# Attention and experts on one core: the last 64 tokens of q and k turned by four transposes, five additions moved behind the mean scores, 34 unread products added

## The chip, the cores and the metric

One core of a Trainium2 chip runs the whole program. The metric is device time in microseconds (us) for one execution, the median over runs. TensorE is called PE here, VectorE DVE, ScalarE ACT, GpSimd POOL and SyncE SP. SP computes nothing in this kernel; it issues most of the transfers between HBM and on-chip memory.

## The reference, cut to what matters

For 8 batches of 8 heads, 576 tokens of 64 elements each, in float32:

```
q_d, k_d, v_d = means of q, k, v over groups of 4 tokens        # 144 groups
out_d  = softmax(q_d k_d^T / 8) v_d                             # 144 x 144 per head
out_up = each row of out_d repeated 4 times
out_local = softmax over |i - j| < 4 of (q k^T / 8), times v    # a band
x = (out_up + out_local), as 4608 tokens of 512
route: logits = x w_gate; every token goes to one of 8 experts, 576 tokens each, in order of logit
out[token] = relu(x w1[e]) w2[e]
```

## The kernel before, in words

The attention part works in 36 units of 128 tokens (four windows of 32), eight batches of four and a half units. For each batch, q and k are loaded with tokens on partitions (`nat`, and `natt` for the last 64 tokens of a batch, because 576 = 4 x 128 + 64), and turned on PE so that head elements lie on partitions (`qt`, `kt`). The first 512 tokens go by pieces of four 128 x 128 transposes (`trw`). The last 64 go by `trt`, one piece per batch: `natt` holds 16 groups of four tokens times four head pairs on 64 partitions for q and 64 for k, and eight f32 products with the identity turn it; the profile counts each as two PE instructions (`L360`, 16 of them a batch). Two copies, one for q and one for k, then bring the 256 columns of PSUM into `qt` and `kt` (`L328` on DVE or `L330` on ACT, which alternate or are set by `TRV`).

POOL or DVE forms the sums over four tokens (`gsum`). The mean attention of a batch (`down`) is three score steps s0, s1, s2 (products on PE; on DVE a row maximum, `L387`, and a subtraction, `L389`; on ACT the exponentials, `L395` to `L398`), then three steps t0, t1, t2 of transposes on PE (`L411`), then the products with v. Local attention of a unit is scores (`L554`), transposes (`L577`) and products with v (`L598`). `log_a(u)` adds the mean rows of a unit to its local rows (`L608`, on DVE for units under 27), `store(u)` writes the sum to HBM through SP, and `log_t`, `log_m` make the logits.

The order of all this is written out by hand: every piece has a due time in units, and pieces are emitted in order of due time, so that each engine runs its own instructions in that order. `LOC` gives the lag of each stage behind its unit; the addition of unit u is due at u + 4.425, its store at u + 4.6. The score and transpose steps of the mean attention of a batch are spread over `DW` = 0.15 to 1.9 units behind the batch's first unit, nine steps. The turning pieces of the next batch are spread between them, so that the last-64 piece of batch b stands on PE just ahead of the t0 step of batch b - 1; it is called trt(b) here. Loads on SP are `paced`: each waits for a DVE instruction emitted shortly before it.

The function `keep` issues products of a constant tile that nothing reads. `KEEP` = (36, 46) places 36 of them ahead of the transposes of the first unit and 46 ahead of the first turning piece of batch 1. All of the PSUM tiles of these stages come from one pool of six banks (`g`).

After the attention come routing and the eight experts (from about 246 us of the span on), which the diff does not touch.

Of the kernel before, what the change touches and what calls it, by code (L numbers as in the profile page):

```python
# [6 lines left out]
F32 = mybir.dt.float32  # L7
# [10 lines left out]
B, H, S, D = 8, 8, 576, 64  # L18
HD = H * D
HP = H // 2  # L20
# [6 lines left out]
GM = 128  # L27
GT = G - GM
# [22 lines left out]
FL = 4  # L51
EXS = (3,)
TRV = (2, 6)
FT = 3
FTS = {0: 5}
UF1 = 29
# [9 lines left out]
NG = 6  # L66
# [30 lines left out]
TX = 0.0  # L97
VX = 0.0
NWARM = 13
KEEP = (36, 46)  # L100
EV0 = (0,1)
EVV = ((3, 1, 1), (4, 1, 1), (6, 1, 1))
EN0, EN1 = 19, 28
# [12 lines left out]
class Attention:  # L116
# [109 lines left out]
    def load_nat(self, b, which, hh=None):  # L226

        nc = self.nc  # L230
        src = {"q": self.q, "k": self.k, "v": self.v}
        tail = 4 * GM * D
        if which == "t":
            t = self.wk.tile([128, 2, 4, D], F32, name="natt", bufs=1)
            for i, w in enumerate("qk"):
                for j in range(2):
                    nc.sync.dma_start(
                        t[64 * i:64 * i + 64, j].rearrange("p f d -> p (f d)"),
                        bass.AP(tensor=src[w].tensor, offset=src[w].offset + (b * H + j) * S * D + tail,
                                ap=[[4 * D, GT], [2 * S * D, HP], [1, 4 * D]]))  # L240
        elif which == "w":
            t = self.wk.tile([128, 4, D], F32, name="natw", bufs=1)
            nc.sync.dma_start(t.rearrange("p f d -> p (f d)"),
                              bass.AP(tensor=self.v.tensor, offset=self.v.offset + b * H * S * D + tail,
                                      ap=[[S * D, H], [4 * D, GT], [1, 4 * D]]))
        else:
            if (which, b) not in self.nat_:
                self.nat_[which, b] = self.ld.tile([128, H * 4 * D], F32, name="nat").rearrange(
                    "p (h f d) -> p h f d", f=4, h=H)
            t = self.nat_[which, b]  # L250
            h0, h1 = (0, H) if hh is None else (2 * hh, 2 * hh + 2)
            nc.sync.dma_start(t[:, h0:h1].rearrange("p h f d -> p h (f d)"),
                              bass.AP(tensor=src[which].tensor, offset=src[which].offset + (b * H + h0) * S * D,
                                      ap=[[4 * D, GM], [S * D, h1 - h0], [1, 4 * D]]))
        self.nat[which, b] = t
# [97 lines left out]
    def trt(self, b):  # L353

        nc = self.nc
        src = self.nat["t", b]
        p = self.ps.tile([128, 4, 2, GT, HP], F32, name="g", bufs=NG)
        for f in range(4):
            for s in range(2):
                nc.tensor.matmul(p[64 * s:64 * s + 64, f].rearrange("p w g h -> p (w g h)"), src[:, s, f], self.ident,  # L360
                                 start=True, stop=True)
        for i, w in enumerate("qk"):
            t = self.dest(b, w)[:, :, 4 * GM:].rearrange("p h (g f) -> p f g h", f=4)
            self.evac(t, p[:, :, i], i, b in TRV)

    def down_s(self, b, part):
        nc = self.nc  # L370
# [31 lines left out]
    def down_t(self, b, part):  # L402
        nc = self.nc
        self.need(("d", b, part))
        t = self.sd
        if part == 0:
            self.ptd[b] = self.wk.tile([128, 11, 128], F32, name="ptd", bufs=1)
        out = self.ptd[b]
        p = self.ps.tile([128, 512], F32, name="g", bufs=NG)
        for j in range(3):  # L410
            nc.tensor.transpose(p[:, 128 * j:128 * j + 128], t[:, 3 * part + j, :GM], self.ident)  # L411
        self.evac(out[:, 3 * part:3 * part + 3].rearrange("p a b -> p (a b)"), p[:, :384], vector=(b, part) == (0, 1))
# [262 lines left out]
    def run(self, after, ready):  # L675
# [15 lines left out]
        for b in range(B):  # L691
            u0, up = 9 * b // 2, 9 * (b - 1) // 2
            t = self.transposes(b)
# [36 lines left out]
        for u in range(NT):  # L730
# [5 lines left out]
            for j, (name, lag) in enumerate(LOC.items()):  # L736
# [9 lines left out]
                    at += {"t": TX, "v": VX, "v0": VX, "v1": VX}.get(name, 0.0)  # L746
                if name == "add" and u == NT - 1:
                    continue
                if name == "st" and u >= NT - XB:
                    at = max(at, STE + 0.001 * u)  # L750
                if name == "up":
# [899 lines left out]
```

## Time and profile before

| what | value |
|---|---|
| median of 3 runs (lowest to highest) | 690.15 us (687.77 to 691.06) |
| time of the profiled execution | 690.15 us |
| its span, first to last instruction | 688.2 us |
| PE, DVE, ACT, POOL busy share of the span | 94%, 74%, 49%, 36% |
| mean granted clock of PE | 0.979 |
| PE products, and as many weight loads | 8843 |

The profiled execution has the time of the median. Busy shares are averages over stages that have different limits, and a busy PE is not PE at its peak: one matmul shows as 0.27 us or so, while four transposes in a row follow one another in less than half a microsecond. A batch's stretch of the attention part is read from the chain of waits and from the timeline instead.

### The profile page before, as it was taken

The numbers are of one execution on the slowest core, as the hardware profiler recorded it, in microseconds if no ns is written. First come the engines' busy times: TensorE is split into PE (matmuls) and PEld (weight loads), VectorE is DVE, ScalarE is ACT, GpSimd is POOL, SyncE is SP. The second block draws the span as 40 slices with busy tenths as digits, with TensorE's granted clock in tenths as the row PEclk, the third lists the DMA queues.
The fourth block names the chain that finished last, engine by engine and source line by source line (L and its number), as shares of the span: only waits on it lengthen the run. The fifth ranks groups of instructions, "written<-read, shape, count | busy, mean of one in ns | idle before, by whom it ended". The sixth has DMA issues, their size and how long they took to land.

```text
span 688.2 us, 21717 instructions
## 1 busy us (share of the span) xinstructions
PE 646.8 (94%) x8843; PEld 453.2 (66%) x8843; DVE 511.8 (74%) x1475; ACT 333.8 (49%) x648; POOL 248.8 (36%) x332
## 2 busy tenths in 40 slices
PE   7899999989999957999999999999999999999993
PEld 4677888778787845765764764764764764755841
DVE  5787889869879987997888897896896966534500
ACT  4677877678586513525325434424424424433410
POOL 4797486656937413106005104103114026111011
PEclk9999999999999967999999999999999999999997
DMA  8978879877987724506439268068078089623001
GB/s 250 241 195 235 232 188 254 222 194 190 232 230 172 222 72 123 193 13 227 144 118 288 48 221 208 25 245 184 24 259 170 25 280 262 224 47 92 1 31 39
DMA packets 132620, 113.90 MB, mean 165 GB/s; under 512 B 81191, under 2 KB 110119, under 8 KB 132521
## 3 DMA queue, kind: packets, MB, share of 16 engines
q1 hardware_dynamic: 124760, 89.71, 46.7%
q0 software_dynamic: 6752, 22.03, 10.1%
q8 instruction: 70, 1.15, 0.7%
q10 hardware_dynamic: 1008, 0.77, 0.4%
q14 instruction: 30, 0.24, 0.1%
HBM read 85.94 MB, written 19.46 MB: 153 GB/s over the span
## 4 chain that ended last, share of the span: by engine, by line
PE 55%; issue 17%; DVE 13%; ACT 4%; POOL 4%; DMA 3%; SPq 1%; POOLq 0%; ACTq 0%; DVEq 0%
PE pX L1439 17%; PE pH L1391 13%; PE g L598 4%; PE g L346 3%; PE s L554 2%; PE pR L934 2%; PE g L577 2%; POOL out_dram L1449 2%; PE g L618 2%; DVE wl L1310 2%; POOL xg L1327 1%; DMA nat<-in_q_dram 1%; DVE qt L328 1%; PE g L427 1%; PE g L411 1%
## 5 line engine op out<-in xcount | busy, mean ns | idle before, releaser
L1391 PE MATMUL pH<-xt,wh 128*128 128x320 f16 (+2 forms) x1040 | 191.8, 284 | 0.3 <-ACT xt L1348 0.2
L1439 PE MATMUL pX<-wh,ht 128*128 128x512 f16 (+1 forms) x640 | 178.9, 380 | 0.0
L1391 PE MATMUL pH<-xt,wl 128*128 128x320 f16 (+2 forms) x520 | 144.4, 284 | 0.1
L1439 PEld LDWEIGHTS <-ht 128*128 128x128 f16 (+1 forms) x960 | 82.9, 100 | 93.4 <-issue 2.6
L1439 PE MATMUL pX<-wl,ht 128*128 128x512 f16 (+1 forms) x320 | 117.9, 380 | 0.0
L1391 PEld LDWEIGHTS <-wh 128*128 128x128 f16 x1040 | 98.1, 97 | 28.2 <-issue 4.1
L1449 POOL DMA_INDIRECT out_dram<-y,idx x40 | 42.1, 1052 | 172.7 <-ACT y L1446 116.1
L1422 ACT ACTIVATE ht<-pH 128x512 f16<-128x512 f32 (+1 forms) x128 | 45.5, 408 | 114.3 <-PE pH L1391 114.3
L1310 DVE SCALAR_TENSOR_TENSOR wl<-nat,wh 128x512 f16<-128x512 f32 x128 | 83.6, 686 | 15.5 <-ACT wh L1307 13.3
L1446 ACT ACTIVATE y<-pX 128x512 f32<-128x512 f32 (+1 forms) x40 | 23.8, 595 | 102.8 <-PE pX L1439 55.0
L1425 DVE SCALAR_TENSOR_TENSOR ht<-pH,ht 128x512 f16<-128x512 f32 (+1 forms) x128 | 52.4, 450 | 25.6 <-ACT ht L1422 25.1
L1307 ACT ACTIVATE wh<-nat 128x1024 f16<-128x1024 f32 (+1 forms) x68 | 67.6, 1002 | 4.5 <-DMA nat<-in_moe_w_dram 4.5
L1327 POOL DMA_INDIRECT xg<-x_dram,idx x40 | 43.6, 1090 | 62.9 <-DVE idx L1220 48.6
L1391 PEld LDWEIGHTS <-wl 128*128 128x128 f16 x520 | 50.1, 97 | 12.6 <-DVE wl L1310 0.3
L587 ACT COPY pt<-g 64x512 f32<-64x512 f32 x71 | 41.2, 580 | 22.8 <-PE g L577 21.8
L598 PE MATMUL g<-vw,pt 128*64 128x65 f32 x1152 | 43.4, 225 | 2.5 <-issue 1.3
L598 PEld LDWEIGHTS g<-vw,pt 128*64 128x64 f32 x1152 | 37.9, 137 | 8.6 <-issue 5.2
L346 PE MATMUL g<-ident,nat 128*128 128x128 f32 x256 | 39.0, 278 | 2.5 <-DMA nat<-in_q_dram 2.0
L1094 POOL MEMSET f<- 128x1 bf16 x8 | 0.8, 104 | 110.9 <-DVE sumf L988 41.1
L330 ACT COPY kt<-g 64x512 f32<-64x512 f32 (+1 forms) x58 | 36.5, 630 | 7.8 <-PE g L346 6.7
L1356 DVE SCALAR_TENSOR_TENSOR xs<-xg,xs 128x512 f16<-128x512 f32 (+1 forms) x30 | 20.1, 688 | 24.8 <-ACT xs L1355 24.6
L554 PE MATMUL s<-kt,qt 64*32 64x38 f32 x2304 | 29.0, 204 | 5.8 <-issue 5.2
(242 smaller groups left out, 1131.4 us busy)
## 6 DMA issues: line engine op xcount, KB each, us to landing
nat<-in_moe_w_dram SPq DMA_DIRECT2D x28, 1024.0 KB
vw<-in_v_dram SPq DMA_DIRECT2D x136, 78.0 KB
x_dram<-x SPq DMA_DIRECT2D x36, 256.0 KB
nat<-in_q_dram SPq DMA_DIRECT2D x32, 256.0 KB
nat<-in_k_dram SPq DMA_DIRECT2D x32, 256.0 KB
nat<-in_v_dram SPq DMA_DIRECT2D x28, 256.0 KB
up<-up_dram SPq DMA_DIRECT2D x9, 256.0 KB
nat<-in_moe_w_dram POOLq DMA_DIRECT2D x2, 1024.0 KB, 8.7
```

The costliest lines, as they stand in the source:

```text
L346: nc.tensor.transpose(p[:, a, :, fp], src[:, 4 * hh + 2 * a + s, 2 * fp:2 * fp + 2].rearrange("p f d -> p (f d)"), self.ident)
L554: nc.tensor.matmul(sv[32 * hp:32 * hp + 32, i, c], qt[r, hp, QW * w:QW * w + QW], kt[r, hp, key0(w):key0(w) + KW], start=False, stop=True, ...
L587: first = nc.scalar.copy(out[r, :, :, a], src)
L598: nc.tensor.matmul(o[64 * i:64 * i + 64, 65 * h:65 * h + 65], pt[:, 2 * (h % 2) + i, 2 * g + h // 2].rearrange("p b q -> p (b q)"), self.v ...
L1307: self.wh.append(nc.scalar.activation(hi[:, a:b], r[:, a:b], AF.Copy, scale=sc))
L1310: self.wl = nc.vector.scalar_tensor_tensor(lo[:, a:a + LOP], r[:, a:a + LOP], sc, hi[:, a:a + LOP], op0=OP.mult, op1=OP.subtract)
L1327: self.fetched = nc.gpsimd.indirect_dma_start(out=xg[:n], out_offset=None, in_=self.x, in_offset=bass.IndirectOffsetOnAxis(ap=idx[:n, c:c ...
L1391: mm = nc.tensor.matmul(p[:, s, o:o + s1 - s0], w[d][a][:, 128 * f:128 * f + 128], xt[:, b, d, s0:s1], start=j == 0, stop=j == len(seq) - 1)
L1422: last = nc.scalar.activation(hi, q, AF.Relu)
L1425: low = nc.vector.scalar_tensor_tensor(lo, q, 0.0, hi, op0=OP.max, op1=OP.subtract)
L1439: mm = nc.tensor.matmul(p[o:o + m], ht[:, f, h0:h0 + m], w[4 + f // 2][b][:, 512 * (f % 2):512 * (f % 2) + 512], start=j < parts, stop=j > ...
L1449: i = nc.gpsimd.indirect_dma_start(out=self.out, in_=y[:n], in_offset=None, out_offset=bass.IndirectOffsetOnAxis(ap=idx[:n, c:c + 1], axis=0))
```

## The change

Four things change.

- The layout of `natt`: 64 tokens of q on partitions 0 to 63 and 64 of k on 64 to 127, eight heads of 64 elements along the free dimension. It is loaded by two transfers of 512 pieces of 256 bytes, where there were four transfers of 64 pieces of 1 KB.
- `trt` turns it by four 128 x 128 transposes, one for each head pair, and the two copies read runs of 64 consecutive columns and write runs of 64, where they read and wrote single elements with strides before.
- For the units 5, 9, 14, 18 and 23 the addition and the store are due 0.17 units later. The addition was due between the score steps s1 and s2 of the mean attention that runs at that time; it is now emitted behind s2's maximum and subtraction.
- `KEEP` gets a third number: 34 unread products stand ahead of the t1 transposes of batch 0.

```diff
+ADD = {5: 0.17, 9: 0.17, 14: 0.17, 18: 0.17, 23: 0.17}
-KEEP = (36, 46)
+KEEP = (36, 46, 34)
...
         if which == "t":
-            t = self.wk.tile([128, 2, 4, D], F32, name="natt", bufs=1)
+            t = self.wk.tile([128, H, D], F32, name="natt", bufs=1)
             for i, w in enumerate("qk"):
-                for j in range(2):
-                    nc.sync.dma_start(
-                        t[64 * i:64 * i + 64, j].rearrange("p f d -> p (f d)"),
-                        bass.AP(tensor=src[w].tensor, offset=src[w].offset + (b * H + j) * S * D + tail,
-                                ap=[[4 * D, GT], [2 * S * D, HP], [1, 4 * D]]))
+                nc.sync.dma_start(t[64 * i:64 * i + 64],
+                                  bass.AP(tensor=src[w].tensor, offset=src[w].offset + b * H * S * D + tail,
+                                          ap=[[D, S - 4 * GM], [S * D, H], [1, D]]))
...
-        p = self.ps.tile([128, 4, 2, GT, HP], F32, name="g", bufs=NG)
-        for f in range(4):
-            for s in range(2):
-                nc.tensor.matmul(p[64 * s:64 * s + 64, f].rearrange("p w g h -> p (w g h)"), src[:, s, f], self.ident,
-                                 start=True, stop=True)
+        p = self.ps.tile([128, HP, 2, S - 4 * GM], F32, name="g", bufs=NG)
+        for hp in range(HP):
+            nc.tensor.transpose(p[:, hp].rearrange("p w s -> p (w s)"), src[:, 2 * hp:2 * hp + 2].rearrange("p h d -> p (h d)"),
+                                self.ident)
         for i, w in enumerate("qk"):
-            t = self.dest(b, w)[:, :, 4 * GM:].rearrange("p h (g f) -> p f g h", f=4)
-            self.evac(t, p[:, :, i], i, b in TRV)
+            self.evac(self.dest(b, w)[:, :, 4 * GM:], p[:, :, i], i, b in TRV)
...
         p = self.ps.tile([128, 512], F32, name="g", bufs=NG)
+        if (b, part) == (0, 1):
+            self.keep(p, 2)
...
+                if name in ("add", "st"):
+                    at += ADD.get(u, 0.0)
```

## Rows read from the trace of the kernel before

**Rows 1.** The page: PE's granted clock in 40 slices; the instruction queue's packets, MB, share.

```profile
PEclk9999999999999967999999999999999999999997
...
q8 instruction: 70, 1.15, 0.7%
```

**Rows 2.** Chain of waits, 157 to 167 us (start, duration, what): two turning pieces.

```profile
161.00 0.44 PE g L346 x4
...
162.31 1.02 PE g L360 x16
```

**Rows 3.** Groups by form, 0 to 230 us: copies of 256 columns out of PSUM.

```profile
L330 ACT COPY kt<-g 128x256 f32<-128x256 f32 x4 | 2.7, 672 | 0.3 <-DVE kt L328 0.3
...
L328 DVE COPY kt<-g 128x256 f32<-128x256 f32 x4 | 2.5, 626 | 0.0
...
L330 ACT COPY ptd<-g 128x256 f32<-128x256 f32 x6 | 2.3, 376 | 0.0
...
L328 DVE COPY ptd<-g 128x256 f32<-128x256 f32 x2 | 0.8, 424 | 0.0
```

**Rows 4.** Timeline, 13 to 24 us: trt(0)'s follower, trt(1), and SP's issues for it.

```profile
14.67 0.57 PEld L554 LDWEIGHTS s<-kt,qt 64*32 64x32 f32 x54 [0.70 <-ACT kt L330]
...
18.88 1.23 SPq L237 DMA_DIRECT2D natt<-in_k_dram  x2
...
22.64 0.19 PEld L360 LDWEIGHTS g<-ident,natt 128*64 128x64 f32 x2 [0.48 <-DMA natt<-in_q_dram]
...
23.25 0.85 PEld L360 LDWEIGHTS g<-ident,natt 128*64 128x64 f32 x14 [0.42 <-issue]
```

**Rows 5.** Timeline of SP, 26 to 30 us: one load of 312 pieces of 256 bytes.

```profile
27.43 0.31 SPq L277 DMA_DIRECT2D vw<-in_v_dram  x1
```

**Rows 6.** Windows (busy us and count per engine; last: clock, DMA share, GB/s).

```profile
5.00:8.00 3.00, 1.50 (x10) 0.88 (x8) 0.02 (x1) 0.00 (x0) 2.93 (x10) 1.00 1.08 366
...
26.00:28.00 2.00, 2.00 (x23) 1.69 (x22) 1.90 (x6) 1.25 (x2) 1.84 (x3) 1.00 1.16 209
```

**Rows 7.** Timeline, 45 to 48 us: trt(2) on PE.

```profile
45.76 0.19 PEld L360 LDWEIGHTS g<-ident,natt 128*64 128x64 f32 x2 [0.51 <-PE g L384]
...
46.63 0.85 PEld L360 LDWEIGHTS g<-ident,natt 128*64 128x64 f32 x14 [0.69 <-issue]
```

**Rows 8.** Chain of waits, 73 to 82 us: what released t0 behind trt(3).

```profile
77.74 0.63 ACT kt L330
...
78.41 0.55 PE g L411 x3
```

**Rows 9.** Timeline, 104 to 107 us: DVE's subtraction of s2, and t1 behind trt(4).

```profile
105.64 0.61 DVE L389 TENSOR_TENSOR sd<-g,mxd 128x432 f32<-128x432 f32 x1
...
106.36 0.31 PEld L411 LDWEIGHTS g<-ident,sd 128*128 128x128 f32 x3 [0.42 <-ACT kt L330]
```

**Rows 10.** Timeline, 164 to 167 us: DVE's last copy of trt(6), and t2.

```profile
165.17 0.62 DVE L328 COPY kt<-g 128x256 f32<-128x256 f32 x1
...
165.91 0.31 PEld L411 LDWEIGHTS g<-ident,sd 128*128 128x128 f32 x3 [0.31 <-ACT sdt L398]
```

**Rows 11.** Timeline, 192 to 197 us: the addition, and t2 behind trt(7).

```profile
192.77 0.68 DVE L608 TENSOR_TENSOR x<-x,g 128x512 f32<-128x512 f32 x1
...
196.65 0.31 PEld L411 LDWEIGHTS g<-ident,sd 128*128 128x128 f32 x3 [0.38 <-ACT sd L395]
```

**Rows 12.** Windows from the start to the first and last of five stops of PE.

```profile
0.00:19.25 19.25, 13.70 (x219) 9.01 (x219) 9.59 (x21) 8.39 (x14) 8.77 (x26) 1.00 0.86 252
...
0.00:184.65 184.65, 168.71 (x3965) 138.27 (x3966) 147.44 (x372) 132.28 (x264) 125.95 (x192) 1.00 0.83 221
```

**Rows 13.** Who waited for whom on PE, 12 to 245 us (us, times, longest us).

```profile
PE s L554 <- issue: 5.2, 4, 1.8
```

**Rows 14.** Timeline: 46 unread products, and t1 of batch 0.

```profile
19.55 1.64 PE L774 MATMUL g<-wm 128*64 128x64 bf16 x46
...
33.52 0.31 PEld L411 LDWEIGHTS g<-ident,sd 128*128 128x128 f32 x3 [1.32 <-ACT sd L395]
```

## The prediction

> **What bounds the kernel now.** I read the page first, then the chain of waits through the attention part, then the timeline around each of the eight last-64 pieces. The clock line of the page shows full clock through the first fourteen slices, which is the whole attention part [rows 1], so nothing there is waiting to be won by a faster PE clock. The chain says that in most stretches PE runs its pieces back to back: in the stretch of trt(6) four transposes take 0.44 us and the sixteen instructions of the last-64 piece 1.02 us, each beginning where the one before ends [rows 2]. A microsecond taken off PE there is a microsecond off the end. But next to three of the eight pieces PE's next step is released by something else: a copy on ACT behind trt(3) [rows 8], and the same at 135 us behind trt(5), or a load ahead of trt(1) and trt(2) [rows 4, 7]. A saving on PE there only lengthens the wait. So each batch has to be worked out by itself.
>
> **The piece on PE.** Sixteen instructions become eight, in four pairs of load and product of the form of a turning piece: 1.02 - 0.44 = 0.58 us less per batch [rows 2], at most 8 x 0.58 = 4.6 us.
>
> **The copies.** Today a copy of 256 columns with strides takes 672 ns on ACT and 626 ns on DVE; the copies of 256 consecutive columns take 376 and 424 ns [rows 3]. The new copies read and write runs of 64, which no row shows. The bounds are the two pairs of rows; I take the lower end, since both sides of the copy are then runs and not single elements: 0.30 us less per copy on ACT, 0.20 on DVE, two copies a batch. Where these engines are not waited for, this is worth nothing.
>
> **The loads.** SP issues four transfers a batch now, two in 1.23 us [rows 4], so some 2.4 us. A load of 312 pieces of 256 bytes issues in 0.31 us when nothing stands in the way [rows 5]; two of 512 pieces I estimate between 0.6 and 1.2 us. SP waits for its pacing most of the time, so I count this only where trt waits for its load. The transfers themselves get dearer. Windows price both forms: 366 GB/s with pieces of 1 KB alone, 209 GB/s in a window with many pieces of 256 bytes, both with the queues full [rows 6]. For the 256 KB of a batch that is 0.72 against 1.25 us, so 0.5 us more. Early, with the transfer engines full, this takes back most of what SP's quicker issue gives; later the load has several microseconds of lead.
>
> The Trainium skill, DMA: Bandwidth & Descriptors, in its table at the head, asks for at least 512 bytes a piece for line rate and says that smaller ones are read, modified and written; it speaks against this edit. The windows agree in sign: the small pieces move at 209 instead of 366. By that rule, taken as twice the time, I estimate 1.4 us for a batch in place of 0.72.
>
> **The additions.** An addition takes 0.68 us of DVE [rows 11], and moved behind s2 it lets s2's subtraction, the exponentials behind it and t2 come that much sooner. The store on SP goes with it, past the transposes' due times; it waits for the addition anyway and the logits of the unit come a whole unit later, so I price the delay of the addition at nothing (if the store held up the paced loads behind it on SP, by 0.68 and the 0.61 us of a subtraction [rows 9] or so, the loads would have to have less lead than that; only trt(1) and trt(2) show a late one, and neither stands beside a moved addition).
>
> **Batch by batch.**
> - trt(0): the scores behind it wait 0.70 us for copies of other pieces, on ACT [rows 4]. PE's saving is lost: 0, at most 0.2 if the last-64 copy is the one that counts.
> - trt(1): its first load is 0.48 us late and the second stop is 0.42 us [rows 4]. Fewer issues bring the load forward, fuller queues set it back. If it lands as now, the piece still ends 0.58 us sooner; with both waits gone, 1.5 us; with the load 0.9 us later (0.45 for each of two batches), -0.3. I take 0.7.
> - trt(2): the stops are 0.51 and 0.69 us [rows 7], the second for the last of the four loads; with two issues in place of four, SP is through sooner and that wait should go. Up to 0.58 + 1.2 = 1.8; but the same two copies on ACT that release t0 behind trt(3) stand here too, and t0 may wait for them next. I take 0.6.
> - trt(3) and trt(5): t0 starts as the ACT copy ends [rows 8], so PE's saving turns into wait; the shorter copies come behind it. 0 to 0.2 each, together 0.1.
> - trt(4): t1 stands 0.42 us behind DVE's subtraction of s2, which ends at 106.25, and ACT's copies [rows 9]. The addition moved lets that end at 105.57, the copies end 0.6 sooner, and PE is 0.58 sooner: I take 0.6.
> - trt(6): t0 and t1 can start sooner only as far as ACT's exponentials let them; t2 waits 0.31 us, as DVE's copy ends (165.17 + 0.62 = 165.79) [rows 10]. That copy ends 0.4 sooner with both copies short: 0.3 of 0 to 0.9.
> - trt(7): t2 waits 0.38 us for exponentials behind s2 [rows 11]; s2 moves up by 0.68, and PE comes 0.58 sooner. 0.7.
>
> Sum: 0.7 + 0.6 + 0.1 + 0.6 + 0.3 + 0.7 = 3.0 us.
>
> **The unread products.** 46 of them take 1.64 us [rows 14], 0.036 each, so 34 take 1.2 us. PE stands idle for 1.32 us ahead of that t1 [rows 14], so they cost nothing if they start at once. They write the bank that the transposes then use; if that bank comes free only 0.6 us into the wait, they end late by 0.5. The ACT chain that t1 waits for moves with PE, so the cover stays. I take 0, and keep 0.5 for the range.
>
> **The instruction stream.** The instruction queue moved 70 packets and 1.15 MB [rows 1], 16 KB each, for PE's 8843 weight loads and as many products: one packet for about 256. PE stops five times in the attention part for "issue", four of them inside the dense runs of `L554`, 5.2 us together [rows 13]. Counting weight loads from the start, the first stop ends at load 219 and the fifth at 3966 [rows 12]: 3747 apart, 30 times 124.9. All five lie on this grid of about 125 loads (250 instructions and some waits), so these are stops at the end of a fetched block, where a dense run eats it up before the next has come. The change takes 12 loads out at each trt and puts 34 in at batch 0, so the code slides along the grid by -12, -24, +10, -2, and so on to -62. Other places meet the ends of blocks; about as many of them lie in dense runs. I take no change, with 2.5 us either way.
>
> The Trainium skill, Runtime: NRT & Kernel Launch, section Instruction fetch mechanics, has the same 256 instructions a block and says that crossing a block is mostly hidden. The trace differs: 5.2 us of stops in `L554` alone. By that page the slide would change nothing and the sum stays.
>
> **From sum to time.** The profiled execution took 690.15 us with a span of 688.2, so 1.95 us lie outside. It equals the median of the runs. 690.15 - 3.0 = 687.15; rounded, 687.0.
>
> **The rivals.**
> - Part of the gain, as summed: 687.0, within 684.5 to 689.5. Chance 0.50.
> - All of it arrives: PE is the bound everywhere, 4.6 us for the pieces, 1.0 for half of the 2.1 us of stops in trt(1) and trt(2), 1.0 for t1 and t2 (0.42 + 0.31 + 0.38, less a little): 6.6, so 683.5. For it: the chain is mostly PE. Against it: rows 8. Chance 0.22.
> - Almost nothing: DVE and ACT set the pace beside all pieces and the saving turns into waits; 0.7 us, 689.5. For it: rows 8 and 10; against it: t2 at trt(7) [rows 11] is held by the very addition that moves. Chance 0.14.
> - The load comes late: the small pieces cost 0.7 us more per batch and set trt(1) and trt(2) back by 0.7 us each in place of gaining 1.3: 687.0 + 1.3 + 1.4 = 689.7. The full queues of the early part speak for it [rows 6], the lead of the later loads against it. Chance 0.06. This is what the Trainium skill's rule of 512 bytes, cited above, would do.
> - Slower: the slide puts more ends of blocks into dense runs. One such stop costs up to 1.8 us [rows 13]. Two more eat the 3.0 us up; from four more on it is slower: 687.0 + 4 x 1.7 = 693.8. There are 36 dense runs, one a unit, and 3966 / 125 = 32 ends by the fifth stop, so it can happen. Chance 0.08.
>
> **How the numbers follow.** About 0.5%, 3.45 us, is what a measurement of this kernel can tell from no change: its three runs span 3.3 us. Faster by more means under 686.7: the second case and a little under half of the first, 0.22 + 0.22 = 0.44. Slower by more means over 693.6: 0.07, most of the last case. The rest is 0.49. The range runs from 682.8, which leaves out the lower end of the second case, to 691.0, which leaves out the last; 2 in 10 or a little less lie outside.
>
> **What would show it.** In the profile after: the last-64 piece with eight PE instructions a batch, near 0.45 us; its copies near 0.4 us; no load wait ahead of trt(2); t2 behind trt(7) without its wait; t0 behind trt(3) still released by ACT; the 34 products inside the wait ahead of t1, which stays at the exponentials; stops for "issue" at other loads, still on a grid of 125. The prediction is wrong if the waits named fail to swallow PE's saving, if the stops change by more than two, or if the last-64 loads land late.

## The result, and the profile after

The change makes the kernel slower: median 692.15 us against 688.97 for the kernel before, 22 runs each on the same chips; ratio 1.0051, 95% interval 1.0033 to 1.0068. The forecast was 687.0, within 682.8 to 691.0. Ratios here and below leave out runs that took over 1.5% longer than the fastest of their kernel (here one of 22, at 700.90 us), so they differ a little from the quotient of the medians.

The profiled execution of the changed kernel took 696.69 us with a span of 694.9, which is 6.7 us more span than in the profile of before, and lies near the upper end of its runs. So sizes below are read from several traces or from medians, and this one trace only says where to look. The page of the changed kernel, to be held against [rows 1]:

```profile
PEclk9899999999999966999999999999999999999998
...
q8 instruction: 69, 1.13, 0.7%
```

The clock line has a new dent in its second slice, and the low stretch after the attention lies across two slices as before. The queue of instructions moved one packet less, as the shorter code asks.

**What came as forecast.** Groups by form, 0 to 230 us, of the changed kernel: the copies of the last-64 piece.

```profile
L327 DVE COPY qt<-g 128x256 f32<-128x256 f32 x4 | 1.7, 418 | 0.0
L327 DVE COPY kt<-g 128x256 f32<-128x256 f32 x4 | 1.7, 414 | 0.0
L329 ACT COPY kt<-g 128x256 f32<-128x256 f32 x4 | 1.5, 380 | 0.0
L329 ACT COPY qt<-g 128x256 f32<-128x256 f32 x4 | 1.5, 370 | 0.1
```

370 to 380 ns on ACT and 414 to 418 on DVE: at the lower bound of [rows 3], which the forecast took. Timeline of PE's weight loads, changed kernel, around pieces 2, 4, 5 and 7 and the unread products:

```profile
34.72 1.15 PEld L772 LDWEIGHTS <-wm 128*64 128x64 bf16 x34 [0.17 <-issue]
35.91 0.31 PEld L407 LDWEIGHTS g<-ident,sd 128*128 128x128 f32 x3
...
48.40 0.42 PEld L358 LDWEIGHTS g<-ident,natt 128*128 128x128 f32 x4 [0.23 <-issue]
...
107.24 0.62 PEld L594 LDWEIGHTS g<-vw,pt 128*64 128x64 f32 x16 [0.37 <-DVE sd L383]
108.46 0.58 PEld L594 LDWEIGHTS g<-vw,pt 128*64 128x64 f32 x16 [0.60 <-PE g L594]
109.10 0.31 PEld L407 LDWEIGHTS g<-ident,sd 128*128 128x128 f32 x3
...
135.49 0.42 PEld L358 LDWEIGHTS g<-ident,natt 128*128 128x128 f32 x4 [0.23 <-issue]
136.90 0.31 PEld L407 LDWEIGHTS g<-ident,sd 128*128 128x128 f32 x3 [0.99 <-ACT kt L329]
...
194.30 0.42 PEld L358 LDWEIGHTS g<-ident,natt 128*128 128x128 f32 x4 [0.23 <-issue]
194.69 0.36 PEld L407 LDWEIGHTS g<-ident,sd 128*128 128x128 f32 x3
196.01 1.08 PEld L594 LDWEIGHTS g<-vw,pt 128*64 128x64 f32 x32 [0.96 <-ACT kt L329]
197.16 0.31 PEld L407 LDWEIGHTS g<-ident,sd 128*128 128x128 f32 x3
```

The piece is four loads and four products, 0.42 us of loads, where there were sixteen of each. The 34 products take 1.15 us, and t1 behind them starts without a wait, where it had waited 1.32 [rows 14]. The load waits of piece 2 [rows 7] are gone. Behind piece 4 the wait ahead of t1 [rows 9] is gone, but two new ones of 0.37 and 0.60 us stand ahead of it within the products with v. The step behind piece 5 now waits 0.99 us for the copies on ACT, and behind piece 7 the wait ahead of t2 [rows 11] is gone while a new one of 0.96 us for copies stands ahead of the products with v.

**What came otherwise.** PE's weight loads from unit 1 to unit 2, the two units' masks (`identb`) being the first and the last line:

```profile
17.56 0.10 PEld L541 LDWEIGHTS <-identb 64*128 64x128 bf16 x2 [0.17 <-issue]
17.73 0.64 PEld L550 LDWEIGHTS s<-kt,qt 64*32 64x32 f32 x63
21.54 0.13 PEld L550 LDWEIGHTS s<-kt,qt 64*32 64x32 f32 x1 [3.17 <-issue]
25.90 0.70 PEld L358 LDWEIGHTS g<-ident,natt 128*128 128x128 f32 x4
...
33.36 0.10 PEld L541 LDWEIGHTS <-identb 64*128 64x128 bf16 x2 [0.23 <-issue]
```

The same in the kernel before:

```profile
17.58 0.10 PEld L545 LDWEIGHTS <-identb 64*128 64x128 bf16 x2 [0.17 <-issue]
...
19.32 0.18 PEld L554 LDWEIGHTS s<-kt,qt 64*32 64x32 f32 x14 [1.03 <-issue]
...
31.01 0.10 PEld L545 LDWEIGHTS <-identb 64*128 64x128 bf16 x2 [0.22 <-issue]
```

Unit 1 begins when it did before (17.56 against 17.58 us). Its 64 scores stop ahead of the last one for 3.17 us; in the kernel before they stopped ahead of the last fourteen, for 1.03. Unit 2 begins 2.35 us later than before (33.36 against 31.01). Windows of the changed kernel over the same stretch (columns as in [rows 6]; the last three are clock, DMA share, GB/s):

```profile
18.00:20.00 2.00, 0.49 (x52) 0.37 (x30) 0.00 (x0) 0.89 (x2) 1.85 (x4) 0.88 1.01 310
20.00:22.00 2.00, 0.46 (x7) 0.38 (x7) 0.14 (x1) 0.00 (x0) 0.01 (x1) 0.50 0.79 158
22.00:24.00 2.00, 2.00 (x42) 2.00 (x40) 1.93 (x4) 0.00 (x0) 0.00 (x0) 0.50 0.92 286
24.00:26.00 2.00, 2.00 (x16) 1.94 (x15) 0.00 (x0) 0.50 (x1) 1.78 (x3) 0.50 0.82 246
```

While PE stands still its granted clock falls from 2.4 GHz to half, 1.2 GHz, and stays there for 6.8 us, to 26.4. The stop itself is 2.1 us longer than before, which is nearly all of the 2.35; what the half clock adds was not separated, since in the kernel before PE waits for loads in the same stretch [rows 4]. The waits of PE from 12 to 245 us, changed kernel, against [rows 13]:

```profile
PE s L550 <- issue: 8.3, 7, 3.0
```

Seven stops and 8.3 us in the score line, where there were four and 5.2. That line alone misleads: in the kernel before a fifth long stop, 1.22 us, stands in the products with v. Counting all lines, each of the two traces has five stops of more than 0.8 us, 6.9 us in sum before and 7.9 after, and behind unit 1 they fell from 5.8 to 4.7. From unit 2 to the last unit's mask the changed kernel is 0.3 us quicker than before (203.45 against 203.74 us), and from there to the end 4.6 us slower. In this trace the loss lies in two places, then, unit 1 and the end, and between them the gain that was forecast is missing.

### The profile page after: what moved, and what is told of

It is laid out like the page before. It is cut to its first block, busy times and chain, and to the rows that moved or that the text cites. A ratio compares the mean times of both kernels' runs of the same rounds, so it can differ in the third digit from the quotient of the medians.

```text
span 694.9 us, 21574 instructions
## 1 busy us (share of the span) xinstructions
PE 648.2 (93%) x8781; PEld 454.9 (65%) x8781; DVE 511.0 (74%) x1475; ACT 332.2 (48%) x648; POOL 246.0 (35%) x332
## 4 chain that ended last, share of the span: by engine, by line
PE 58%; issue 18%; DVE 12%; ACT 6%; POOL 3%; DMA 2%; another core or an unknown queue 0%; POOLq 0%; SPq 0%; DVEq 0%; ACTq 0%
PE pX L1437 17%; PE pH L1389 14%; PE g L594 4%; PE g L345 3%; PE s L550 3%; PE g L573 3%; PE pR L932 2%; POOL out_dram L1447 2%; PE g L614 2%; DVE wl L1308 1%; DMA nat<-in_k_dram 1%; POOL xg L1325 1%; PE g L423 1%; DVE qt L327 1%; PE g L428 1%
## 5 line engine op out<-in xcount | busy, mean ns | idle before, releaser
L1447 POOL DMA_INDIRECT out_dram<-y,idx x40 | 40.5, 1011 | 179.4 <-ACT y L1444 119.3
```

What stands on the lines that cost most here:

```text
L1447: i = nc.gpsimd.indirect_dma_start(out=self.out, in_=y[:n], in_offset=None, out_offset=bass.IndirectOffsetOnAxis(ap=idx[:n, c:c + 1], axis=0))
```

## The experiments

All ratios are to the kernel before, run on the same chip. Four theories stand in the expectations, which are quoted as written: **A**, the place of PE's instructions in the stream sets the time, through stops at the ends of fetched blocks and the clock that falls behind them; **B**, the loads in small pieces come late or take the queues; **C**, the saving was never there; **W**, only work and waits set the time, not places. A "slide" of n means that an instruction of PE (weight loads, products and semaphore instructions counted) stands n places later than in the kernel before. The new piece is 25 instructions shorter, so each batch slides the rest by about -25; the 34 products slide it by +68.

**The four parts.** The new layout, loads, transposes and copies alone (`p1_trt`); the moved additions alone (`p2_add`); the 34 products alone (`p3_keep34`); everything but the 34 (`p4_nokeep`).

```diff
 # p1_trt, against the kernel after
-ADD = {5: 0.17, 9: 0.17, 14: 0.17, 18: 0.17, 23: 0.17}
+ADD = {}
-KEEP = (36, 46, 34)
+KEEP = (36, 46)
 # p4_nokeep: only the second; p2_add: only the first, in the kernel before
 # p3_keep34, against the kernel before
-KEEP = (36, 46)
+KEEP = (36, 46, 34)
```

> Only the new layout, its two loads and the four transposes; additions and unread products as before. Theory A (ends of fetched instruction blocks): PE's saving is real, 2 to 3 us, and is eaten by stops at block ends, which grow by 1 to 3 us because the same blocks now hold denser code: between 1.5 us faster and 1 us slower than before, and the sum of stops for 'issue' in the attention part is above that of before by 1 us or more. Theory B (the loads of small pieces come late and hold everything up in the first 30 us): the whole loss is here, 3 us slower, with unit 2 starting 2 us later than before. Theory C (the saving never existed, ACT and DVE set the pace): equal to before within 0.5 us, with stops as before.

> Only the five additions and stores moved. No PE instruction is added or taken away, so by theory A the block ends stay where they are: 0.5 to 1.0 us faster (the waits of t1 behind trt(4) and t2 behind trt(7) go). By theory C 0. If the moved stores hold up loads behind them on SP, slower by up to 1 us.

> Only the 34 unread products. If they sit in an idle wait of 1.3 us they cost nothing themselves: by theories B and C equal to before within 0.5 us. By theory A they slide all later PE code by 68 instructions along the blocks of 256: stops change by some 2 us, by a count on the blocks of before to the worse, so 1 to 3 us slower. If the products end late, 0.5 us slower from there on, with stops as before.

> The whole change without the 34 unread products. Theory A: the block ends fall elsewhere than in the whole change from unit 3 on, so the time differs from it by 1 to 3 us, either way; theory B: as slow as the whole change, 3 us slower than before; if the products were what cost the time, 1 to 3 us faster than before.

| | ratio | interval |
|---|---|---|
| `p1_trt` | 1.0113 | 1.0066 to 1.0159 |
| `p2_add` | 1.0019 | 0.9992 to 1.0046 |
| `p3_keep34` | 1.0084 | 1.0057 to 1.0112 |
| `p4_nokeep` | 1.0095 | 1.0061 to 1.0129 |

The additions, which leave PE's instructions in their places, do nothing that can be told from zero. The other three, which slide them, are all slower. `p3_keep34` is the plainest: its 34 products stand inside a wait and cost nothing where they are (the next unit begins as in the kernel before), all loads, copies and turning pieces are those of before, and still it loses 0.84%. Some 90 us behind the products, the weight loads of that kernel, and behind them its windows:

```profile
123.68 0.18 PEld L556 LDWEIGHTS s<-kt,qt 64*32 64x32 f32 x3 [2.39 <-issue]
```

```profile
120.00:123.00 3.00, 1.42 (x75) 1.19 (x73) 1.37 (x5) 1.31 (x3) 2.77 (x4) 1.00 0.92 225
123.00:125.00 2.00, 1.32 (x8) 1.04 (x8) 0.91 (x3) 0.00 (x0) 1.85 (x6) 0.54 0.42 107
125.00:129.90 4.90, 4.90 (x114) 4.05 (x114) 2.75 (x9) 2.22 (x4) 4.43 (x7) 0.50 0.75 196
```

A stop three loads ahead of the end of a score run, then half clock to 129.9 us. W falls with this run: no work was added to the path and no wait that names another engine.

That these stops are the ends of blocks, the traces show in two ways. Counting PE's instructions in each of the twenty traces (loads, products and semaphore instructions), 78 of the 79 stops for "issue" of more than 0.8 us in the attention part come ahead of an instruction whose number leaves 194 or 195 when divided by 256, whatever code stands there. And at the first of these places PE runs on 1.3 to 1.7 us behind the landing of a packet of 16 KB on the instruction queue, in all twenty.

**The slide by itself.** Unread products at the very start, where PE only warms up, slide everything behind them and add next to nothing (in both slid versions of the kernel before, unit 2 begins at 30.4 us, in the unslid one at 29.9 and 31.0): 32 products slide by 64, 64 of them (with three of the warming products left out) by 122. In the kernel before (`s1_before32`, `s2_before64`) and in the one after (`s3_after32`, `s4_after64`):

```diff
-NWARM = 13
+NWARM, NSLIDE = 13, 32        # or 10, 64
...
+        for _ in range(NSLIDE):
+            self.nc.tensor.matmul(p[:64, :64], w[:, :64], w[:, :64], start=True, stop=True)
```

> The kernel before with 32 unread products behind the warm-up products, in PE's wait for its second load: 64 instructions more ahead of everything, no work added or taken away behind them. Theory A (block ends, and the clock that falls behind a long stop): another time than before by 1 us or more, to the slower side if the place of before is a lucky one, with stops on the same grid of 256 instructions at other code. Theory W (the edits' own work and waits set the time, stops are a small matter): equal to before within 0.5 us, at most 1 us slower if the products delay the first pieces.

> The kernel before with 64 unread products and 10 warm-up products for 13: a slide of 122 instructions, nearly half a block. Theory A: another time than before and than the slide of 64, by 1 us or more, with the block ends of unit 1 away from its scores. Theory W: equal to before within 1 us.

> The whole change slid by 64 instructions in the same way. Theory A: its time moves by 1 us or more against the unslid change (3.5 us slower than before); if the stop in unit 1 goes, it is within 1 us of before or faster. Theory W: 3.5 us slower than before, as unslid.

> The whole change slid by 122 instructions. Theory A: the end of the block that stopped unit 1 now falls into the unread products ahead of it, which run at 36 ns a pair and give the fetch more time, so the stop of 3.3 us and the half clock behind it go: 1 to 4 us faster than the unslid change. Theory W: 3.5 us slower than before.

| | ratio | interval |
|---|---|---|
| `s1_before32` | 1.0067 | 1.0038 to 1.0096 |
| `s2_before64` | 1.0047 | 1.0022 to 1.0073 |
| `s3_after32` | 1.0006 | 0.9977 to 1.0035 |
| `s4_after64` | 1.0022 | 0.9994 to 1.0049 |

The same work in another place of the stream costs the kernel before as much as the whole change does, and gives the changed kernel some of its loss back (clear of the noise in `s3_after32` alone). A holds; C and W do not explain this. That a slide would take the stop of unit 1 away was wrong: in `s4_after64` the score run stops ahead of 62 of its 64 products instead:

```profile
19.94 0.64 PEld L550 LDWEIGHTS s<-kt,qt 64*32 64x32 f32 x62 [1.65 <-issue]
```

The stop is shorter but has not gone. Slides can't be chosen by looking at one place.

**Padded back, with controls.** Twelve unread products ahead of each last-64 piece, without the 34, so that PE's instructions stand within five places of where they stood, counted in the traces (`q1_pad64`: 64x64 products; `q2_pad32`: 32x8). Beside them the kernel before against itself (`q3_before_again`) and the changed kernel once more (`q4_after_again`).

```diff
         p = self.ps.tile([128, HP, 2, S - 4 * GM], F32, name="g", bufs=NG)
+        f = p.rearrange("p h w s -> p (h w s)")
+        for _ in range(12):
+            nc.tensor.matmul(f[:64, :64], self.wm[:, :64], self.wm[:, :64], start=True, stop=True)
```

> The change without the 34 products (which measured 0.95% slower than before), with 12 unread products of 64 x 64 ahead of each of the eight last-64 turnings: 24 PE instructions each, so that all other code stands within some 12 instructions of its place in before, block by block. Theory A (block ends): although PE does 12 x 0.036 = 0.43 us more work a batch, it is 4 to 8 us faster than without the products, and between 2 us faster and 1 us slower than before. Theory W (work and waits): the products add up to 3.5 us to the unpadded kernel, so 1.0 to 1.5% slower than before.

> The same with products of 32 columns by 8, which should take less of PE's time. Theory A: as with 64 x 64 or faster by up to 1.5 us, since half of the work comes back: 0 to 4 us faster than before. Theory W: 0.9 to 1.2% slower than before.

> The kernel before, unchanged, run like the others. Both theories: a ratio of 1.000 within 0.002. If it came out at 1.003 or more, the losses of the slid kernels would be a matter of how they are run. Its profile tells how much stops and half-clock stretches move from one execution to the next: theory A expects the large stops at the same code as in the first profile.

> The whole change, unchanged, on this chip: 0.3 to 0.7% slower than before by its first measurement. Theory A: its large stops at the same instructions as in its first profile (end of the first block within unit 1's scores, near 62 us, and three in a row at 176 to 187 us), and the half clock in unit 1 if that stop is again over 2 us.

| | ratio | interval |
|---|---|---|
| `q1_pad64` | 1.0041 | 1.0011 to 1.0071 |
| `q2_pad32` | 1.0031 | 1.0006 to 1.0055 |
| `q3_before_again` | 0.9997 | 0.9971 to 1.0023 |
| `q4_after_again` | 1.0070 | 1.0037 to 1.0102 |

The padded kernels do more work on PE than `p4_nokeep` (1.0095) and lose less than half as much. But 0.3 to 0.4% were left that A does not account for.

**The rest.** The new loads alone (`t1_loads`): the kernel before, its `natt` filled by the two transfers of 256-byte pieces and turned by the old products, so that the elements of the last 64 tokens stand in a wrong order and the work is the same; PE's instructions are those of before but for up to five semaphore instructions. Then the padding made as exact as it can be (within four places), 12 or 13 products in turn, with the additions moved (`t2_pad_exact`) and without (`t3_pad_exact_noadd`).

```diff
 # t1_loads, against the kernel before: in place of the two transfers of 64 x 1 KB
+                nc.sync.dma_start(t.rearrange("p j f d -> p (j f) d")[64 * i:64 * i + 64],
+                                  bass.AP(tensor=src[w].tensor, offset=src[w].offset + b * H * S * D + tail,
+                                          ap=[[D, S - 4 * GM], [S * D, H], [1, D]]))
 # t2_pad_exact, against q1_pad64 (t3_pad_exact_noadd: and ADD = {})
-        for _ in range(12):
+        for _ in range(12 + b % 2):
```

> The kernel before with nothing but the last-64 loads changed: two transfers of 512 pieces of 256 bytes in place of four of 64 pieces of 1 KB, into the same tile. PE's instructions, the copies and the waits are those of before; the old products read the tile in the wrong layout, so the order of elements in the last 64 tokens is wrong and the work is the same. A (block ends and the clock): ratio 1.000, 0.998 to 1.002; stops for issue in the attention part 7 to 9.5 us, at the places of before. B (small pieces take the queues and come late, or set back the fetches of instructions): ratio 1.003 to 1.004, that is what the padded versions still lost, with load waits ahead of the piece of batch 1 or 2 or longer stops.

> The whole change without the 34 products, and 12 or 13 unread 64x64 products in turn ahead of the last-64 piece of each batch, so that PE's instructions stand at their index of before to within one or two through the whole attention part. A: stops and clock as before, PE's work as before too (12 products of 0.036 us take up the 0.58 us saved), and what is left is the shorter copies, the quicker issue and the additions: ratio 0.995 to 1.000. If 1.002 to 1.004 again, as with 12 a batch, something other than the place of the blocks costs 2 us or more: the loads (then the run with the loads alone shows it) or the moved additions (then the run without them does not have it).

> The same without the moved additions: new layout, loads, transposes and copies, PE's instructions at their index of before. A: 0.996 to 1.001. B: 1.003 as far as the loads alone cost it. If the additions are what costs, this is 0.003 below the version with them.

| | ratio | interval |
|---|---|---|
| `t1_loads` | 1.0038 | 1.0008 to 1.0068 |
| `t2_pad_exact` | 1.0019 | 0.9987 to 1.0050 |
| `t3_pad_exact_noadd` | 0.9998 | 0.9970 to 1.0026 |

B is right as well: the loads alone cost 0.38%, though the interval comes close to nothing. And `t3_pad_exact_noadd` is `p1_trt` with 12 or 13 useless products a batch put in: 0.9998 against 1.0113. Adding work took 1.1% off.

So the loads ran again (`u2_loads_again`), as did the exact padding (`u3_pad_again`), and beside them a version with the padding of batches 2 to 7 ahead of the t0 transposes, where PE waits in several batches (`u1_pad_late`):

```diff
 # u1_pad_late, against t3_pad_exact_noadd
-        for _ in range(12 + b % 2):
+        for _ in range(0 if b > 1 else 12 + b):
...
         p = self.ps.tile([128, 512], F32, name="g", bufs=NG)
+        if part == 0 and 0 < b < 7:
+            for _ in range(13 - b % 2):
+                nc.tensor.matmul(p[:64, :64], self.wm[:, :64], self.wm[:, :64], start=True, stop=True)
```

> The exactly padded version without the moved additions, with the 12 or 13 unread products of batches 2 to 7 not ahead of the last-64 piece but ahead of the t0 transposes that follow it on PE, where PE waits in several batches for the copies of that piece. A: PE's instructions stay at their places, and up to 0.45 us a batch of the padding goes into waits: ratio 0.995 to 0.999, below the version with the padding ahead (0.9998) by 0.001 to 0.003. W (what PE saves at that piece is swallowed by other waits): the same as with the padding ahead, 0.998 to 1.002.

> The kernel with the loads alone in pieces of 256 bytes once more (wrong order of elements in the last 64 tokens, the same work). If the 0.4% of the first time belongs to the loads, 1.002 to 1.006 again; if it was scatter, 0.998 to 1.002.

> The exactly padded version without the moved additions once more, beside the one with the padding late: 0.997 to 1.003. If the loads cost 0.4%, the shorter copies and the earlier last-64 piece pay it back here; if this comes out above 1.005, the first value was scatter and the place of the instructions is not enough.

| | ratio | interval |
|---|---|---|
| `u1_pad_late` | 1.0006 | 0.9982 to 1.0029 |
| `u2_loads_again` | 1.0032 | 1.0011 to 1.0054 |
| `u3_pad_again` | 1.0015 | 0.9985 to 1.0045 |

The loads cost 0.3 to 0.4%, twice. With PE's instructions in place, the version with all the new work in it (0.9998, 1.0015) can't be told from the kernel before although it carries those loads, so the shorter copies and whatever else is left of the change may pay part of them back; the intervals overlap, and this is not shown. Padding late instead of early brings nothing. No version beats the kernel before.

**Where the loads are paid.** Timeline of the weight loads in `u2_loads_again`:

```profile
17.71 0.10 PEld L543 LDWEIGHTS <-identb 64*128 64x128 bf16 x2 [0.17 <-issue]
...
19.62 0.17 PEld L552 LDWEIGHTS s<-kt,qt 64*32 64x32 f32 x13 [1.20 <-issue]
22.69 0.20 PEld L344 LDWEIGHTS g<-ident,nat 128*128 128x128 f32 x2 [0.64 <-DMA nat<-in_k_dram]
24.89 0.88 PEld L358 LDWEIGHTS g<-ident,natt 128*64 128x64 f32 x16 [2.00 <-issue]
...
32.69 0.10 PEld L543 LDWEIGHTS <-identb 64*128 64x128 bf16 x2 [0.23 <-issue]
```

The stop in the score run is near that of before, but the piece of batch 1 starts at 24.89 us, 1.6 to 2.3 us later than the two parts of it with the old loads (22.64 and 23.25 [rows 4]), behind a late load of `nat` and 2.00 us of standing. The stretch from unit 1's mask to unit 2's, in all traces whose instructions stand in place up to there or slide by -25:

| loads, place of the instructions | traces | us from unit 1 to unit 2 |
|---|---|---|
| old, in place (before, `q3`, `p2`, `p3`) | 4 | 13.43, 13.66, 13.43, 13.53 |
| new, in place (`t1`, `t2`, `t3`, `u1`, `u2`, `u3`, `q1`, `q2`) | 8 | 14.27 to 15.93, mean 14.83 |
| new, 25 earlier (after, `q4`, `p1`, `p4`) | 4 | 15.80, 16.28, 15.48, 15.61 |

No trace overlaps between the first two rows. By the means the loads cost 1.3 us there (1.9 in `t1` and `u2`, which change nothing else), the slide 1.0 us more. In the four traces of the last row the score run stops for 2.8 to 3.3 us, in the eight of the middle row for 1.2 to 2.2, in the four of the first for 1.0 to 2.0. The half clock is not what divides the rows: six of the eight in the middle one have it here, but `u2` (14.98 us) and `q1` (14.50) do not.

What does go with a stop's length there is the order on SP. In the twelve traces in place, the stop lasts 2.0 to 2.2 us in the four where SP issued two loads of `natt` for batch 1 ahead of the start of the instruction packet (`p2`, `t1`, `t2`, `q2`), and 1.0 to 1.6 in the eight where the packet came first; in the four that slide by -25 both loads came first as well. No run set that order on purpose, so what is cause and what effect stays open.

**Where the gain went.** Where no stop or late load falls, a unit takes the same time in every trace to within a few hundredths of a microsecond, so the units that hold pieces 2 to 7 show what the change is worth there (us from a unit's mask to the next):

| piece, its unit | forecast gain | old piece and loads (`before`, `q3`, `p2`, `p3`, `s1`, `s2`) | new loads alone (`t1`, `u2`) | new, with additions moved (`after`, `q4`, `p4`, `s3`, `s4`) | padded, additions not moved (`t3`, `u3`) |
|---|---|---|---|---|---|
| 2, unit 4 | 0.6 | 8.07 to 8.74 | 7.66, 7.67 | 7.66 to 7.88 | 7.66, 7.66 |
| 3, unit 9 | 0.1 with piece 5 | 8.76 to 9.08 | 8.78, 8.76 | 8.61 to 8.62 | 8.63, 8.63 |
| 4, unit 13 | 0.6 | 9.01 to 9.02 | 9.02, 9.01 | 9.01 to 9.02 | 9.02, 9.01 |
| 5, unit 18 | see piece 3 | 8.44 to 8.56 | 8.44, 8.45 | 8.88 to 8.89 | 8.44, 8.45 |
| 6, unit 22 | 0.3 | 8.42 to 8.45 | 8.42, 8.43 | 8.17 to 8.23 | 8.14, 8.14 |
| 7, unit 27 | 0.7 | 8.88 to 8.89 | 8.89, 8.89 | 8.88 to 8.89 | 8.88, 8.89 |

From least to least, the changed kernel gains 0.41 + 0.15 + 0.25 us and loses 0.44, 0.4 in all where 2.3 were booked. The 0.41 comes with the new loads alone. The gains at pieces 3 and 6 are not in the kernels with the loads alone, but they are in the padded one, where unread products take up most of what the shorter piece saves; that leaves the copies. PE's shorter piece brings no gain in any of these units, nor do the moved additions: in unit 18 the two together cost 0.44 us (8.45 in `p1_trt` without the additions, 8.44 in `p2_add` with them alone). For this part of the question C is right.

## Why the prediction was wrong

Three terms of the sum failed: the instruction stream, put at no change; the load of batch 1, put at a gain of 0.7 us; and the gain at pieces 2 to 7, put at 2.3 us and measured at 0.4. The first and second made the kernel slower, the third left nothing to set against them.

**The instruction stream: the step that failed.** "... about as many of them lie in dense runs. I take no change, with 2.5 us either way." The grid was read rightly, and the slides were worked out. But the runs with a slide and nothing else cost 0.47% and 0.67%, 3.3 and 4.6 us, and the 34 products alone 0.84%, 5.8 us: outside those 2.5 us on the wrong side. Two things were missing from the term. First, a stop's length was taken to be up to 1.8 us, as [rows 13] show it; after the change one of them is 3.17 us: the block's end met the run of scores one load ahead of its end instead of fourteen, and the next block's packet came later, for a reason that was not found. The packet of 16 KB lies between 16 and 18 us in the trace of before and between 18.7 and 20 in the one after. Second, a stop can have a sequel that no row of before showed: half clock for 3.4 to 6.8 us. It is not a mark of slid kernels alone, though: `q3`, the kernel before run again, has 3.4 us of it in the attention part, and so have most of the versions in place. Over all traces, the stops of more than 0.8 us on the grid of blocks take 2.5 to 6.9 us, mean 4.3, in the eleven that stand within five places of before, and 4.5 to 12.1, mean 7.5, in the nine that slide. The rival nearest to this ("more ends of blocks into dense runs") stood at 0.08 and counted four more stops of 1.7 us; in the changed kernel there are five and four (`q4`) where the kernel before has five, but one of them is of 3 us.

The kernel before seems to be no fair draw of places, either: all three slides of it that were tried were slower (`s1`, `s2`, `p3`). The forecast took places to be as good as one another.

**The loads: the second miss.** "Early, with the transfer engines full, this takes back most of what SP's quicker issue gives", and 0.7 us of gain was booked for batch 1. SP's quicker issue came, in the timeline of SP of the changed kernel:

```profile
17.55 0.64 SPq L237 DMA_DIRECT2D natt<-in_q_dram  x1
18.24 0.64 SPq L237 DMA_DIRECT2D natt<-in_k_dram  x1
```

1.3 us for a batch, a little over the upper end of the estimate of 0.6 to 1.2. The transfers took back more than that: 1.3 us lost between unit 1 and unit 2, 2.2 to 2.6 us (0.32 and 0.38% of 689) over the whole. The rival for this gave 2.7 us and a chance of 0.06. At piece 2 the loads did bring the gain that was expected of them: unit 4 is 0.4 us shorter with the new loads alone. The rule of the Trainium skill that was weighed there, DMA: Bandwidth & Descriptors, table at the head, spoke against this edit, and the runs agree with its sign: at 256 bytes a piece the loads alone are slower (1.0032 and 1.0038). In the windows of before the difference was already priced (366 against 209 GB/s [rows 6]); the step that went wrong was the cover that was assumed for it.

**The piece on PE and the copies: in form as forecast, in worth not; the third miss.** Four loads and four products (the forecast counted loads and products together after the change, eight, but products alone before, sixteen), copies at 370 to 418 ns, no load wait ahead of piece 2, t2 behind piece 7 without its wait. As forecast too, part of it turns into waits for ACT's copies, 0.99 us behind piece 5 (0.57 before). But the waits that the forecast saw go were followed by new ones ahead of the products with v: 0.60 us behind piece 4, where 0.6 us of gain were booked, and 0.96 behind piece 7, where 0.7 were booked. Units 13 and 27 are as long as before. Of the 2.3 us that were booked for pieces 2 to 7, 0.4 are there, and none of it is PE's shorter piece.

**The additions.** 1.0019 alone, and 1.0019 with against 0.9998 without in the padded pair: nothing that can be told from zero, with no sign of the gain that was booked with them for batches 4 and 7 (units 13 and 27 again).

**The unread products: nothing, as forecast, where they stand.** Their slide is what they cost.

**The end.** From the last unit's mask to the last instruction, 453.5 us in the kernel before and 458.0 in the changed one. The last unit's mask in the weight loads of the changed kernel, and behind it windows of that kernel:

```profile
236.81 0.10 PEld L541 LDWEIGHTS <-identb 64*128 64x128 bf16 x2 [0.17 <-issue]
```

```profile
246.00:272.00 26.00, 15.18 (x195) 10.67 (x193) 19.51 (x85) 4.74 (x11) 2.70 (x10) 0.54 0.21 66
...
279.00:282.40 3.40, 3.40 (x31) 3.33 (x29) 2.48 (x8) 2.09 (x5) 0.87 (x2) 0.51 0.87 296
```

The same stretch in the kernel before:

```profile
279.00:282.40 3.40, 3.40 (x44) 2.55 (x42) 2.30 (x10) 2.19 (x5) 0.00 (x0) 1.00 0.98 355
```

The clock comes back at 272.1 us (267.3 in the kernel before) and is low once more at 279 to 282, when the experts have begun; the kernel before runs at full clock there. Over all traces the stretch from the last unit's mask to the end goes with the slide: 453.5 to 457.5 us, mean 454.6, in the twelve whose instructions stand within five places of before in the last unit (`s4_after64` is one, as its slide has run out there), 456.4 to 459.7, mean 458.0, in the eight that stand 63 to 198 places off. By the means, this is the largest piece of the loss. In the profiled execution 0.8 of its 4.6 us lie ahead of the first product of the routing, and 3.2 between the experts' first product with w1 and their first with w2, where the clock is low once more; in `q4`, the same kernel, it is 4.1 and 1.5 (of 6.1). The later return of the clock by itself costs little: from the first product of the routing to the first of the experts the changed kernel takes 27.2 us and the kernel before 27.0. Why the places differ from one execution to the next was not found.

**What stays open.** When the fetch of a block starts was not found, so a slide's cost can't be worked out ahead from these traces: of the expectations, those that did so missed. Whether the small pieces also delay the fetches, or only the loads of `nat` and `natt` behind them, was not tried apart. No version has the new piece unpadded and its instructions in good places; by the units above, PE's 0.58 us a batch would bring nothing there either in batches 2 to 7.

## What to carry to other kernels

In a kernel of dense runs of small products, an edit that changes the number of an engine's instructions moves every later block end; test it with the count padded back, and a slide with nothing else beside it, before the edit itself is judged. A few stops for "issue" on a regular grid in the profile of before are a price that any such edit can raise by several microseconds, and a range must hold that on the slow side above all. A load's shorter issue is no gain where the transfer engines are full: price the pieces by the windows, and ask for the lead that would hide them. And follow a saving to the start of the next unit: a wait that goes is worth nothing if the next piece waits in its place.

## What the runs showed of the hardware

The stop at a block's end can be as long as 3.31 us in a run of 64 loads that otherwise takes 0.64 (`p1_trt`, unit 1), and PE's granted clock then falls to 1.2 GHz. In the twenty traces, every stretch of half clock that begins between 12 and 242 us begins within such a stop or at most 1.8 us behind one. A long stop alone does not decide that: in `p2_add` the same place stops for 2.04 us and the clock stays at 2.4 GHz, in `t3_pad_exact_noadd` a stop of 1.22 us goes with a fall. The stop in `p1_trt`, then the stop and windows of the other two:

```profile
20.71 0.10 PEld L550 LDWEIGHTS s<-kt,qt 64*32 64x32 f32 x1 [3.31 <-issue]
```

```profile
19.16 0.18 PEld L555 LDWEIGHTS s<-kt,qt 64*32 64x32 f32 x14 [2.04 <-issue]
```

```profile
18.00:20.00 2.00, 0.84 (x33) 0.80 (x34) 0.45 (x1) 0.00 (x0) 0.79 (x3) 1.00 1.02 321
20.00:22.00 2.00, 2.00 (x42) 1.79 (x38) 1.62 (x4) 0.35 (x1) 0.17 (x1) 1.00 0.99 305
```

```profile
18.15 0.18 PEld L553 LDWEIGHTS s<-kt,qt 64*32 64x32 f32 x13 [1.22 <-issue]
```

```profile
18.00:20.00 2.00, 1.85 (x44) 1.80 (x44) 1.43 (x3) 0.00 (x0) 0.60 (x3) 0.59 1.11 295
20.00:22.00 2.00, 2.00 (x26) 1.93 (x23) 0.64 (x2) 0.00 (x0) 1.14 (x1) 0.55 1.13 206
```

And two transfers of 512 pieces of 256 bytes, in the changed kernel, took SP 0.64 us each to issue, where two of 64 pieces of 1 KB took 1.23 together [rows 4]: eight times the pieces, no longer to issue, dearer to move.
